# Empty TensorE instructions taken out of a fused RWKV6 and shrink layer, and one more pair of tiles joined in block 2

## The chip, the cores and the metric

One core of one Trainium2 chip runs the whole kernel. The metric is the device time of one launch in microseconds (us). Five engines work side by side, each with its own stream of instructions: TensorE (PE) multiplies, its weight loads are listed apart as PEld, VectorE is DVE, ScalarE is ACT, GpSimd is POOL, and SyncE (SP) issues DMAs. A q behind an engine's name (PEq, SPq) is its sequencer.

## The reference, cut to what matters

```python
# attention: B, H, S, D = 4, 8, 768, 48
for t in range(S):
    cur = u * k[t] (outer) v[t]
    y[t] = r[t] @ (state + cur)
    state = w[t][:, None] * state + k[t] (outer) v[t]
x = y as (B*S, H*D)            # 3072 tokens x 384
h = x @ w_in                   # 384 x 2048
g = h - tanh(h)
out = g @ w_out                # 2048 x 384
```

All tensors are float32.

## The kernel before, in words

The 3072 tokens are cut into 8 blocks of 384 (a batch and a half of its sequence). The attention of block i + 1 is worked out while the two dense layers of block i run; block 0's own attention comes first, in a stage of some 25 us. The dense layers of a block are 16 tiles f of 128 hidden units, and the main loop (from L1346) goes over the blocks and the tiles.

A tile, as a rule:
- `first` (L893): three float32 matmuls of 128x384 on PE (L895) into the one PSUM tile `hp`. A float32 matmul runs as two passes on PE, each with its own weight load, so it is four instructions of PE's stream.
- `slight` (L972 and on): for small h, h - tanh(h) is made as a product of two tanh. ACT makes them (L984, L985), and a square that is summed for a later test (L988).
- DVE multiplies them to g (L902) and makes sums and differences of pieces of g (L1007) for the second layer.
- `Fewer.add` (L1088): the second layer, for two tiles (a pair) at a time, as products of 128x128 of such forms. Part 0 of a pair takes products 8, 9, 10, 11, 6, 7, part 1 takes 0 to 5; they are due two and three tiles after the pair's second tile. Of a pair's ten forms DVE makes 0 to 3 at once and holds back 4 to 9 (two in one L1007), which only part 1 needs. Behind a joined pair 1, forms 6 and 7 of pair 0 stand right behind the product g (L902) of tile 3 in DVE's order, and 8 and 9 two places further on.

A pair of tiles can instead be **joined** (`Twos.begin`, L958): eleven float32 matmuls of 128x192 in place of twelve, which need forms of the weights (`weight_forms`, L934, the tile `kept`) and of the block's tokens (`token_forms`, L942, the tile `turned`). Their results are put together by one copy of ACT (L959) and four additions of DVE (L968), and then `slight` runs on both tiles from the SBUF tile `joint`. `JOINED` lists the joined pairs of each block, `PAIRS` and `FORMED` where their weight forms are made: the key is (block, tile), the value the set and the order of its five forms.

Between the tiles stand pieces of the next block's attention. Three of them are bursts of many small matmuls on PE: the scores "earlier" (L504), the "update" of the states (L585), and the results "together" (L781), near the end of each block: 352 or 384 instructions, alternately. The decays of a block are running products along time, made on DVE as scans: "behind" (L439, with `take_whole`, L459), and "before" (L426, L427), each for halves "2" and "0" of the heads. `plan(i)` (L1142 to L1193) says at which tile of block i each of these steps stands: `phases` for PE's steps, `before` for steps of block i + 1, `ahead` for steps of block i + 2, and `loads` for the DMAs, whose issue is made to stand behind the tanh of its tile. In block 0 the k of block 2 is loaded at tile 13 (L379), just ahead of the L781 burst; in blocks 1 and 3 to 5 its r is loaded a tile or two ahead of that burst.

The order of instructions on PE, DVE, ACT and SP is the order in which the program writes them (a manual schedule); only the waits between engines are put in by the framework.

`first` also takes a count `apart`: so many empty instructions (NOP, L898) are put on PE behind each of its matmuls. `SPACED` has two counts for each block, for its tiles up to 12 (13 in blocks 0 and 1) and for those behind. Other empty instructions (L1042) stand in block 0's second layer.

## Time and profile before

| what | value |
|---|---|
| median of 3 runs | 537.61 us (536.98 to 539.62) |
| the profiled execution | 538.27 us, of which the span of the trace is 536.4 us |
| PE's granted clock, mean of the span | 0.995 |
| DVE, ACT busy | 462.5 us (86%), 310.3 us (58%) |
| bytes moved | 56.33 MB, mean 105 GB/s |

Times inside the trace count from the start of the span. The page's line "q8 instruction" is the DMA queue that brings instructions. In a row of a timeline stand the start, the duration, the engine, the line, the operation, what it writes and reads, its shape and the count of equal instructions that were put in one row; in brackets the idle time of the engine before it, and what ended it. A windows row has a stretch, its length, and for each engine the busy time with its count, then the granted clock of PE, the DMA share and GB/s. A DMA answer has 40 digits, the busy share of the 16 DMA engines in 40 equal slots of the stretch asked for (a packet is put where it starts), and the queues' packets, megabytes and share.

### The profile page before, as it was taken

To read this page: it belongs to the slowest core of one execution; us is meant where nothing else is said; L and a number is where in the kernel's file an instruction comes from. 1 tells how busy PE (TensorE), PEld (TensorE's weight loads), DVE (VectorE), ACT (ScalarE), POOL (GpSimd) and SP (SyncE) were. 2 spreads that over 40 slices of the span, in tenths; PEclk is the share of its full clock that TensorE was granted. 3 is DMA by queue.
4 is the path that set the end of the run, shared out by engine and by line. 5 is a ranking of instruction groups with operands and counts; after the bars stand their busy time and mean duration, and the time that the engine had idled before them with its cause. 6 is when DMAs were issued, how large, how long until landed. Compare 5 with 4: busy or idle time off the path is not lost.

```text
span 536.4 us, 14922 instructions
## 1 busy us (share of the span) xinstructions
PE 526.9 (98%) x5950; PEld 437.5 (82%) x5950; DVE 462.5 (86%) x970; ACT 310.3 (58%) x720; POOL 9.1 (2%) x57
## 2 busy tenths in 40 slices
PE   8899999999999999999999999999999999999996
PEld 5756666677887889889789898899888897899994
DVE  7899897699979889988998899988999889667874
ACT  4899984666445573555655475374735655435450
POOL 1100000000000000000000000000000000000001
PEclk9899999999999999999999999999999999999999
DMA  8698733252302622162313722146221510100011
GB/s 280 224 404 333 241 105 109 89 148 61 120 13 89 163 74 89 51 137 82 120 57 75 178 60 68 50 90 165 63 90 39 140 40 2 56 1 2 11 34 47
DMA packets 53046, 56.33 MB, mean 105 GB/s; under 512 B 21488, under 2 KB 50928, under 8 KB 52976
## 3 DMA queue, kind: packets, MB, share of 16 engines
q1 hardware_dynamic: 52592, 55.18, 34.2%
q8 instruction: 49, 0.80, 0.7%
q14 instruction: 21, 0.17, 0.1%
q10 hardware_dynamic: 288, 0.10, 0.1%
q0 software_dynamic: 96, 0.07, 0.1%
HBM read 44.73 MB, written 4.72 MB: 92 GB/s over the span
## 4 chain that ended last, share of the span: by engine, by line
PE 96%; DMA 1%; issue 1%; ACT 0%; DVE 0%; SPq 0%; PEldq 0%; PEld 0%; DVEq 0%
PE acc L1088 27%; PE hp L895 27%; PE att L958 17%; PE acc L1039 6%; PE att L781 4%; PE hp L1088 3%; PE att L1088 3%; PE att L504 3%; PE att L585 2%; PE acc L1066 1%; PE att L895 1%; DMA r<-in_rT 1%; PE acc L895 1%; PE att L527 1%; PE att L689 1%
## 5 line engine op out<-in xcount | busy, mean ns | idle before, releaser
L895 PE MATMUL hp<-xT,w_sb 128*128 128x384 f32 x438 | 154.3, 488 | 0.7 <-issue 0.7
L1088 PE MATMUL acc<-forms,g 128*128 128x128 f32 x972 | 135.9, 276 | 0.0
L1088 PEld LDWEIGHTS acc<-forms,g 128*128 128x128 f32 x972 | 124.0, 192 | 4.3
L895 PEld LDWEIGHTS hp<-xT,w_sb 128*128 128x128 f32 x438 | 78.6, 190 | 43.5 <-issue 0.9
L1007 DVE TENSOR_TENSOR g<-g 128x256 f32<-128x256 f32 x270 | 107.1, 419 | 4.6 <-PE acc L1088 0.3
L984 ACT ACTIVATE h<-hp 128x384 f32<-128x384 f32 x73 | 35.9, 492 | 96.8 <-PE hp L895 96.8
L902 DVE SCALAR_TENSOR_TENSOR g<-h,qa 128x384 f32<-128x384 f32 x112 | 61.7, 551 | 21.8 <-ACT h L988 21.4
L988 ACT ACTIVATE h<-h 128x384 f32<-128x384 f32 x113 | 58.7, 519 | 0.0
L1088 PE MATMUL acc<-w_sb,g 128*128 128x128 f32 x324 | 54.1, 276 | 0.0
L958 PE MATMUL att<-xT,w_sb 128*128 128x192 f32 x250 | 53.0, 326 | 0.0
L1088 PEld LDWEIGHTS acc<-w_sb,g 128*128 128x128 f32 x324 | 46.4, 192 | 5.5
L968 DVE TENSOR_TENSOR joint<-joint,att 128x384 f32<-128x384 f32 (+1 forms) x72 | 34.6, 501 | 18.0 <-PE att L958 11.0
L984 ACT ACTIVATE h<-joint 128x384 f32<-128x384 f32 x36 | 18.7, 518 | 39.7 <-DVE joint L968 39.7
L958 PEld LDWEIGHTS att<-xT,w_sb 128*128 128x128 f32 x250 | 41.4, 190 | 0.0
L985 ACT ACTIVATE qa<-hp 128x384 f32<-128x384 f32 x73 | 35.7, 489 | 0.0
L1123 DVE TENSOR_TENSOR sums<-sums 128x256 f32<-128x256 f32 x84 | 32.9, 410 | 1.4 <-ACT sums L1100 0.9
L1039 PE MATMUL acc<-w_sb,sums 128*128 128x384 f32 x96 | 33.7, 487 | 0.0
L271 ACT ACTIVATE up<-raw 128x768 f16<-128x768 f32 (+1 forms) x32 | 32.7, 1093 | 0.0
L1039 PEld LDWEIGHTS acc<-w_sb,sums 128*128 128x128 f32 x96 | 18.1, 190 | 12.3
L427 DVE TENSOR_TENSOR_SCAN pre<-w,start 128x780 f32<-128x780 f32 x14 | 25.0, 1782 | 0.8
L439 DVE TENSOR_TENSOR_SCAN post<-w,seed 128x780 f32<-128x780 f32 x14 | 24.9, 1775 | 0.0
L958 PE MATMUL att<-turned,kept 128*128 128x192 f32 x126 | 23.9, 326 | 0.0
(157 smaller groups left out, 768.3 us busy)
## 6 DMA issues: line engine op xcount, KB each, us to landing
raw<-in_weights SPq DMA_DIRECT2D x16, 768.0 KB, 6.4
w<-in_wT SPq DMA_DIRECT2D x7, 780.0 KB, 5.4
k<-in_kT SPq DMA_DIRECT2D x7, 768.0 KB, 4.5
r<-in_rT SPq DMA_DIRECT2D x7, 768.0 KB, 4.4
v_sb<-in_v SPq DMA_DIRECT2D x8, 576.0 KB, 4.1
k<-in_tokens SPq DMA_DIRECT2D x7, 576.0 KB, 4.2
r<-in_tokens SPq DMA_DIRECT2D x7, 576.0 KB, 4.9
out_y<-sums SPq DMA_DIRECT2D x18, 128.0 KB, 1.9
```

What stands on the lines that cost most here:

```text
L271: return lambda: nc.scalar.activation(out=to, in_=of, func=AF.Copy, scale=scale, bias=bias)
L895: nc.tensor.matmul(hp, lhsT=w_in_sb[:, f, kc, :], rhs=xT[kc], start=(kc == KC - 1), stop=(kc == 0))
L902: return lambda: nc.vector.scalar_tensor_tensor(out=out, in0=in0, scalar=scalar, in1=in1, op0=op0, op1=ALU.mult)
L958: nc.tensor.matmul(to, lhsT=lhs, rhs=rhs, start=n == 0, stop=n + 1 == len(of))
L968: return [lambda of=of: nc.vector.tensor_tensor(out=of[0], in0=of[1], in1=of[2], op=ALU.add) for of in ((h[:, 0:5:4], twice(h[:, 3]), both ...
L984: made = nc.scalar.activation(out=t, in_=h, func=AF.Tanh, scale=INNER / UPSCALE)
L985: nc.scalar.activation(out=by, in_=h, func=AF.Tanh, scale=OUTER / UPSCALE)
L988: nc.scalar.activation(out=t, in_=t, func=AF.Square, accum_out=top[:, n:n + 1])
L1007: return lambda: nc.vector.tensor_tensor(out=G[:, to:to + 2], in0=two(G, g_at(q, a0), g_at(q, a1)), in1=two(G, g_at(q, b0), g_at(q, b1)), ...
L1039: nc.tensor.matmul(acc, lhsT=g[:, j * P:(j + 1) * P], rhs=w_out_sb[:, f, :], start=(f == self.first), stop=(f == NF - 1))
L1088: nc.tensor.matmul(to, lhsT=G[:, g_at(q, a), :], rhs=rhs, start=start, stop=stop, skip_group_check=True)
L1123: ops.append(lambda op=op, at=at: nc.vector.tensor_tensor(out=at[0], in0=at[1], in1=at[2], op=OPS[op]))
```

## The change

- `SPACED` and the count `apart` go: the 483 empty instructions behind the matmuls of `first` are no longer made. Those of L1042 stay.
- Pair 1 (tiles 2 and 3) is joined in block 2 as well. Its weight forms are made at tile 8 of block 1, those of pair 7 at tile 5 of block 2, and those of pairs 3 and 4, which stood at tile 8 of block 1, at tile 6 of block 2. The token forms of block 2 are made at its tile 0.
- The scan "behind 0" with `take_whole` moves from tile 0 of block 2 to tile 15 of block 1, and the scan "before 2" from tile 2 to tile 1 of block 2. "before 0" stays at tile 3, where it stood.
- In block 2 the phases that split scores are not moved up behind a joined pair (`near and i > 2`).

```diff
-SPACED = (3, 0), (0, 3), (3, 2), (2, 3), (3, 2), (2, 3), (3, 0), (0, 0)
...
-JOINED = {2: (4, 7), 3: BESIDE, 4: BESIDE, 5: BESIDE, 6: BESIDE, 7: TWOS}
+JOINED = {2: (1, 4, 7), 3: BESIDE, 4: BESIDE, 5: BESIDE, 6: BESIDE, 7: TWOS}
 PAIRS = range(1, 2), range(3, 5), range(7, 8)
...
-FORMED = {(1, 8): (1, (0, 2, 1, 4, 3)), (1, 15): (0, (0, 2, 1, 4, 3)), (2, 6): (2, (0, 2, 1, 4, 3)),
+FORMED = {(1, 8): (0, (0, 2, 1, 4, 3)), (2, 5): (2, (0, 2, 1, 4, 3)), (2, 6): (1, (0, 2, 1, 4, 3)),
...
-    def first(xT, f, hp, apart=0):
+    def first(xT, f, hp):
         for kc in reversed(range(KC)):
             nc.tensor.matmul(hp, lhsT=w_in_sb[:, f, kc, :], rhs=xT[kc],
                              start=(kc == KC - 1), stop=(kc == 0))
-            for _ in range(apart):
-                nc.tensor.nop(nofuse=True, hint="apart")
         return hp
...
-            ahead = {12: ("bound 2",), 13: ("behind 2", "take_whole 2"), 14: ("bound 0",)}
+            ahead = {12: ("bound 2",), 13: ("behind 2", "take_whole 2"), 14: ("bound 0",),
+                     15: ("behind 0", "take_whole 0")}
...
-            before = {0: ("behind 0", "take_whole 0", "times_behind 2"), 1: ("times_behind 0",), 2: ("before 2",),
-                      3: ("before 0",), 4: ("times_before", "held"), 5: ("product_u",), 7: ("product_r",),
+            before = {0: ("times_behind 2",), 1: ("times_behind 0", "before 2"), 3: ("before 0",), 4: ("times_before", "held"), 5: ("product_u",), 7: ("product_r",),
...
-                h = first(here, f, to[:, 0:NB], SPACED[i][f > 12 + (i < 2)])
+                h = first(here, f, to[:, 0:NB])
...
-                if near:
+                if near and i > 2:
...
-            if later and i in JOINED and f == (i == 2) or i == blocks_n - 2 and f == 14:
+            if later and i in JOINED and not f or i == blocks_n - 2 and f == 14:
```

Line numbers of the changed kernel are lower: by one from L80 to L895 or so, by three behind `first`.

PE in block 0, the last tile ahead of the L781 burst, which follows four rows further on. Before, each matmul of the first layer is followed by three empty instructions:

```order
L895 MATMUL hp<-xT_134,w_sb 128x384
L898 NO_OP x3
L895 MATMUL hp<-xT_133,w_sb 128x384
L898 NO_OP x3
L895 MATMUL hp<-xT_132,w_sb 128x384
L898 NO_OP x3
L1039 MATMUL acc_131<-w_sb,sums 128x384
L1042 NO_OP
```

The same place of PE's stream now:

```order
L894 MATMUL hp<-xT_134,w_sb 128x384
L894 MATMUL hp<-xT_133,w_sb 128x384
L894 MATMUL hp<-xT_132,w_sb 128x384
L1036 MATMUL acc_131<-w_sb,sums 128x384
L1039 NO_OP
```

Nothing but the empty instructions went, so what follows stands nine places earlier in the stream for each such tile.

PE in block 2, from pair 1 (tiles 2 and 3) to the scores burst. Before, the two tiles and those behind them run one by one; these are the end of tile 4, part 1 of pair 0, tile 5 and the burst (`hp` is written by the first layer, the three `acc` by the second):

```order
L895 MATMUL hp<-xT_1315,w_sb 128x384
L898 NO_OP x3
L1088 MATMUL acc_131<-forms,g 128x128 x4
L1088 MATMUL acc_602<-w_sb,g 128x128
L1088 MATMUL acc_602<-forms,g 128x128
L895 MATMUL hp<-xT_1317,w_sb 128x384
L898 NO_OP x3
L895 MATMUL hp<-xT_1316,w_sb 128x384
L898 NO_OP x3
L895 MATMUL hp<-xT_1315,w_sb 128x384
L898 NO_OP x3
L504 MATMUL att_126<-pre,post 64x64 x24
```

Now, from the end of part 0 of pair 0 on (the eleven matmuls of the joined pair stand six rows ahead of the first row):

```order
L1085 MATMUL acc_602<-forms,g 128x128 x2
L894 MATMUL hp<-xT_1191,w_sb 128x384
L894 MATMUL hp<-xT_1190,w_sb 128x384
L894 MATMUL hp<-xT_1189,w_sb 128x384
L1085 MATMUL acc_131<-forms,g 128x128 x4
L1085 MATMUL acc_602<-w_sb,g 128x128
L1085 MATMUL acc_602<-forms,g 128x128
L894 MATMUL hp<-xT_1191,w_sb 128x384
L894 MATMUL hp<-xT_1190,w_sb 128x384
L894 MATMUL hp<-xT_1189,w_sb 128x384
L503 MATMUL att_126<-pre,post 64x64 x24
```

Part 1 of pair 0 (the three L1085 rows in the middle) stands behind tile 4 and ahead of tile 5, and the scores burst behind tile 5, both as before; ahead of them, eleven shorter matmuls stand in the place of tiles 2 and 3.

DVE, from tile 15 of block 1 into tile 1 of block 2. Before (L902 is the product g of a tile, L1007 its forms):

```order
L902 SCALAR_TENSOR_TENSOR g<-h,qa 128x384
L439 SCALAR_TENSOR_TENSOR post<-w,seed 128x780
L1007 TENSOR_TENSOR g<-g 128x256
L459 TENSOR_SCALAR whole<-post 128x12
L453 TENSOR_TENSOR post<-k,post 128x768
L902 SCALAR_TENSOR_TENSOR g<-h,qa 128x384
L1007 TENSOR_TENSOR g<-g 128x256 x4
L1115 SCALAR_TENSOR_TENSOR sums<-att_125,o 128x384
L453 TENSOR_TENSOR post<-k,post 128x768
L942 TENSOR_TENSOR turned<-xT_1315 128x192
```

Now:

```order
L438 SCALAR_TENSOR_TENSOR post<-w,seed 128x780
L458 TENSOR_SCALAR whole<-post 128x12
L899 SCALAR_TENSOR_TENSOR g<-h,qa 128x384
L452 TENSOR_TENSOR post<-k,post 128x768
L1004 TENSOR_TENSOR g<-g 128x256
L939 TENSOR_TENSOR turned<-xT_1189 128x192
L939 TENSOR_TENSOR turned<-xT_1190,xT_1189 128x192
L939 TENSOR_TENSOR turned<-xT_1190,turned 128x192 x2
L899 SCALAR_TENSOR_TENSOR g<-h,qa 128x384
L1004 TENSOR_TENSOR g<-g 128x256 x4
```

The scan (the row that writes `post` from `w` and `seed`) now stands ahead of the product g of block 1's last tile, in the place of pair 1's weight forms, and the token forms (`turned`) stand a tile earlier.

## The prediction

> **What bounds the kernel now.** I read the page first, then the waits of PE, the timeline around its two holes, the DMA answers of the same moments, and at last the places that the change touches.

> ```profile
> PE 526.9 (98%) x5950; PEld 437.5 (82%) x5950; DVE 462.5 (86%) x970; ACT 310.3 (58%) x720; POOL 9.1 (2%) x57
> q8 instruction: 49, 0.80, 0.7%
> PE 96%; DMA 1%; issue 1%; ACT 0%; DVE 0%; SPq 0%; PEldq 0%; PEld 0%; DVEq 0%
> ```

> PE is busy for 98% of the span and holds 96% of the chain that ended last, so a gain must shorten PE's own work and a loss must open a hole in it. The waits of PE behind the first layer's start show two holes that no engine explains; "issue" means that nothing visible was waited for:

> ```profile
> PE att L504 <- issue: 1.5, 1, 1.5
> PE hp L895 <- issue: 0.7, 1, 0.7
> ```

> The timeline of PE shows the second (start, duration, operation). The L781 burst of block 6 is followed by one pass of tile 13, whose 384 columns last 0.32 us from start to start, and then by nothing until 458.25: about 0.9 us lost.

> ```profile
> 454.18 1.56 PE L781 MATMUL att<-pre,states 48*48 48x64 f32 x96
> 455.56 1.52 PE L781 MATMUL att<-scores,v_sb 64*48 64x64 f32 x96
> 457.01 0.59 PE L895 MATMUL hp<-xT,w_sb 128*128 128x384 f32 x1
> 458.25 1.45 PE L895 MATMUL hp<-xT,w_sb 128*128 128x384 f32 x4 [0.66 <-issue]
> ```

> Ahead of it lies one packet of the instruction queue. The DMA answer for 455.70 to 455.90 (40 slots of 5 ns) has it in slot 20, at 455.80, and 32.0% of 16 engines for 0.2 us are 1.02 us: it ended at 456.82, and PE went on 1.43 us later.

> ```profile
> DMA  0000000000000000000900000000000000000000
> q8 instruction: 1, 0.02, 32.0%
> ```

> The first hole ends in the same way. In 18.50 to 18.70 the packet stands in slot 15, at 18.57; 35.7% of 3.2 us are 1.14 us, so it ended at 19.71, and PE went on at 21.15, which is 1.44 us later.

> ```profile
> DMA  0000000000000090000000000000009990009090
> q8 instruction: 1, 0.02, 35.7%
> ```
> ```profile
> 21.15 0.50 PE L504 MATMUL att<-pre,post 48*64 48x64 f32 x18 [1.51 <-issue]
> ```

> So PE waits for code. 0.80 MB in 49 fetches are 16.4 KB each, and the distance of the two holes says how many instructions that is. Between them the windows view counts 4968 matmul passes and 4969 weight loads, and the two lines of empty instructions (NOP) have all of theirs there:

> ```profile
> 21.15:458.25 437.10, 436.45 (x4968) 357.15 (x4969) 390.03 (x803) 264.57 (x612) 2.69 (x31) 1.00 0.38 113
> L898 PEldq NOP  x483: 13/13/13, 24.3 to 451.3; - x161
> L1042 PEldq NOP  x33: 13/13/13, 31.0 to 74.9; - x33
> ```

> **The law of a page.** The two L781 rows and the L895 row behind them give 2.83 us for 384 instructions (192 passes, 192 loads), 7.37 ns each. Counting, page ends lie at instruction 131 of block 6's burst and just behind its last. PE passed the former at 454.18 + 131 x 0.00737 = 455.15; the page after it could be used at 458.25, 3.1 us later. A page that lies wholly in a burst is eaten in 256 x 0.00737 = 1.89 us, which leaves a hole of 3.1 - 1.89 = 1.2 us. Outside the bursts a pass of 128 columns and its load take 114 ns (24 of them from 291.00 to 293.73 in the rows of part 2), 57 ns an instruction, and a page lasts many times 3.1 us. So only where the page ends lie in the L781 bursts counts. Before, the end that matters is over 30 instructions behind the burst in blocks 2 to 5, and no hole is seen there.

> **Part 1: the 483 empty instructions.** In place they cost PE nothing. Tiles in block 1 (none) and block 2 (three behind each matmul):

> ```profile
> 135.99 2.10 PE L895 MATMUL hp<-xT,w_sb 128*128 128x384 f32 x6
> 137.92 1.05 PE L1088 MATMUL acc<-forms,g 128*128 128x128 f32 x8
> ```
> ```profile
> 176.13 2.10 PE L895 MATMUL hp<-xT,w_sb 128*128 128x384 f32 x6
> 178.07 1.05 PE L1088 MATMUL acc<-forms,g 128*128 128x128 f32 x8
> ```

> From L895 to the next product it is 1.93 us without and 1.94 us with them. What they do is shift the pages. Counted in the new list, page ends fall at these instructions of the bursts: block 0 at 73 and 329 (before: 203); block 1 at 15 and 271; block 2 at 165, and 37 behind its end; block 3 at 176, and 80 behind; block 4 just ahead and at 251; block 5 at 6 and 262; block 6 at 81 and 337.

> Block 6: both ends are now inside, so the hole is 1.2 us where it was 0.9: **+0.3**.

> Block 0: by the law alone +1.2. But the load of k is issued just ahead of this burst:

> ```profile
> 77.91 0.38 SPq L379 DMA_DIRECT2D k<-in_kT  x1
> 78.37 1.56 PE L781 MATMUL att<-pre,states 48*48 48x64 f32 x96
> 79.75 1.52 PE L781 MATMUL att<-scores,v_sb 64*48 64x64 f32 x96
> 81.20 2.20 PE L895 MATMUL hp<-xT,w_sb 128*128 128x384 f32 x6
> ```

> The fetch that belongs to the end at 203 was due at 78.37 + 203 x 0.00737 + 0.65 = 80.5 (0.65 being 455.80 - 455.15). The DMA answer for 81.70 to 81.85 has it in slot 22, at 81.78, where k's packets run out (q1 fills the slots until then):

> ```profile
> DMA  9909000019000100190900900090000000990000
> q8 instruction: 1, 0.02, 39.9%
> ```

> It waited 1.3 us for the bulk load. In the changed kernel the fetch is due at 78.37 + 73 x 0.00737 + 0.65 = 79.6, in the midst of that load; started at 81.78 as well, it ends at 82.75 and is usable at 84.2, while PE needs it at 78.37 + 329 x 0.00737 = 80.8. The hole is **3.4 us**. The ends are 1.2 (no waiting) and 3.4; I take 3.4, since the delayed fetch was seen in this very load.

> Blocks 1, 4 and 5: the first end lies at the burst's start, where each instruction of lead of the sequencer is worth 57 ns, so 22 of them would hide the 1.2 us. But the load of r fills the DMA up to the burst; block 1, 138.60 to 142.60, and its burst:

> ```profile
> DMA  0000000000136619674296999999999999999743
> ```
> ```profile
> 142.63 0.55 PE L781 MATMUL att<-scores,v_sb 64*48 64x64 f32 x24
> ```

> A fetch that starts at the burst's start, behind the load, is usable 1.0 + 1.44 = 2.4 us in; PE needs it after 271, 251 and 262 instructions, at 2.0, 1.85 and 1.93 us. That is 0.4, 0.6 and 0.5, **+1.5** together; the ends are 0 and 3 x 1.2 = 3.6.

> The clock: in the two stretches behind the 1.5 us hole at 20 us, the granted clock (the column behind the count) is about half for some 3.5 us:

> ```profile
> 22.00:24.00 2.00, 2.00 (x64) 0.59 1.04 371
> 24.00:26.00 2.00, 2.00 (x35) 0.56 0.95 361
> ```

> If block 0's hole brings the same, 2.00 x 0.41 + 2.00 x 0.44 = 1.7 us of PE's work is lost. Behind the 0.9 us hole it did not happen. Ends 0 and 1.7; I take the middle, **+0.8**. [...]

> **Part 2: pair 1 joined in block 2.** Block 3 joins the same pair already, and its rows have every step (the timeline of PE, then of DVE):

> ```profile
> 287.42 1.14 PE L958 MATMUL att<-xT,w_sb 128*128 128x192 f32 x6
> 291.00 1.05 PE L1088 MATMUL acc<-forms,g 128*128 128x128 f32 x8
> 293.73 2.10 PE L895 MATMUL hp<-xT,w_sb 128*128 128x384 f32 x6
> 295.76 1.63 PE L504 MATMUL att<-pre,post 48*64 48x64 f32 x96
> 297.32 1.16 PE L1088 MATMUL acc<-forms,g 128*128 128x128 f32 x8
> 296.30 0.56 DVE L902 SCALAR_TENSOR_TENSOR g<-h,qa 128x384 f32<-128x384 f32 x1 [0.21 <-ACT h L988]
> 296.78 1.09 DVE L1007 TENSOR_TENSOR g<-g 128x256 f32<-128x256 f32 x3
> ```

> The joined pair takes 291.00 - 287.42 = 3.58 us against 2 x 1.94 for two tiles: **-0.3**. What comes late is part 1 of pair 0: its third product reads forms that DVE makes behind tile 3's product. The chain runs over the copies, the tanh of both tiles, L902 and the first of the three L1007, which ends at 296.78 + 0.42 = 297.20 (three that start 0.34 apart take 1.09), 9.78 us behind the pair's start. In block 3 the L504 burst of 1.56 us stands between tile 4 and part 1 and hides the wait. In block 2 that burst comes a tile later, so PE arrives at part 1 295.76 - 287.42 = 8.34 us after the start, does two products (four passes of 114 ns, 8.80), and stands until 9.78; the last L1007 ends 0.67 us later, which two more products (0.46) do not cover, 0.2 more. I take **+1.2** (ends 0, if block 2's shorter queues bring the chain forward, and 1.5). Behind the waiting product on PE stand only tile 5 and the L504 burst; nobody else is late for it.

> DVE gets the pair's four L968 (about 2 us), the pair's forms move to other tiles, and the two scans go earlier. The tightest receiver is the second pair of block 2, whose forms are ready at 179.55 and read at 183.66:

> ```profile
> 179.26 0.29 DVE L934 TENSOR_TENSOR kept<-w_sb,kept 128x128 f32<-128x128 f32 x1
> 183.66 1.14 PE L958 MATMUL att<-turned,kept 128*128 128x192 f32 x6
> ```

> The 2 us added ahead of it fit into these 4.1 us, and no DMA moves: 0. Were that cover gone, the price would be what exceeds 4.1 us.

> **The sum:** 3.4 + 1.5 + 0.3 + 0.8 - 0.3 + 1.2 = +6.9 us on the profiled execution's 538.27 us (span 536.4), 545.2. The median shown is 537.61, 0.66 lower, so I predict **544.5 us**.

> **Rivals.**
> Fetches are not held up by loads: block 0 loses 1.2, blocks 1, 4 and 5 nothing, block 6 +0.3, block 2 +0.9, the clock perhaps 0.8. That is +2.4 to +3.2, 540.0 to 540.8. For it speaks that the load of k is issued only just ahead of the fetch; against it, the packet at 81.78.
> Not slower: the sequencer runs so far ahead that all fetches are hidden. Then 0.9 of block 6 goes and block 2's 0.9 comes: 537.6. For block 0 it decides from a lead of about 73 + 22 = 95 instructions. Against it: block 6's end at 131 left a hole of 0.9. [...]
> The empty instructions cost PE time after all: 483 x 13 ns (L898's own row) are 6.3 us, 531.3 us or a little more. Against it: 1.93 beside 1.94.

> **How the numbers follow.** Forecast 0.58, fetches not held up 0.22, hidden 0.15, empty instructions on PE 0.02, worse than all this (a clock lost in several places) 0.03. The forecast's own range is 541.9 to 547.0: all ends of blocks 1, 4 and 5, clock and wait together would give more at either side, but not at once. Reaching to the case of fetches that are not held up, the range is 540.0 to 547.0. A measurement tells about 0.5% from no change, 2.7 us, so "same" is 534.9 to 540.3: 0.15 and a part of the second case.

> **What would show it.** PE's waits list "issue" at L781 in block 0 (about 80.8 to 84.2) and block 6, small ones in blocks 1, 4 and 5, none at L895 behind block 6's burst; a wait of L1088 for DVE g L1007 in block 2 between tiles 4 and 5; a half clock behind block 0's hole or not; each hole ends 1.44 us behind a packet of the instruction queue. Without the L781 holes the count or the law is wrong; with block 0's hole at 1.2 us the hold-up is.

## The result, and the profile after

| | before | changed |
|---|---|---|
| median of 4 runs each, us | 538.26 (536.98 to 539.62) | 545.95 (544.09 to 546.80) |
| profiled execution, us (span) | 538.27 (536.4) | 544.09 (542.4) |
| ratio of the runs | | 1.0138 (1.0100 to 1.0176) |

The change costs 7.7 us between the medians. The profiled execution of the changed kernel is the fastest of its four (the others took 1.8 to 2.7 us longer, at mean granted clocks of 0.991 to 0.995 against its 0.997), so its trace shows less, 6.0 us of span. By the starts of the results bursts (L781, now L780), in the two traces:

| stretch | before, us | changed, us | difference |
|---|---|---|---|
| start to block 0's burst | 78.37 | 76.62 | -1.75 |
| to block 1's | 64.26 | 69.10 | +4.84 |
| to block 2's | 60.32 | 61.65 | +1.33 |
| to block 3's, to block 4's | 125.61 | 125.61 | 0 |
| to block 5's | 62.85 | 63.33 | +0.48 |
| to block 6's | 62.77 | 63.31 | +0.54 |
| to the end of the span | 82.22 | 82.78 | +0.56 |

The first row is no part of the change, whose first removed instruction stands behind block 0's own attention (the boot, some 25 us): the hole at 20 us, 1.5 us before, was 0.4 us in this execution, and no half clock followed it. Without it the rows add up to 7.75 us, close to what the medians show.

The page of the changed kernel, the rows that were shown of before (PE, the instruction queue, the chain):

```profile
PE 527.8 (97%) x5960; PEld 439.5 (81%) x5960; DVE 464.3 (86%) x974; ACT 310.2 (57%) x721; POOL 9.1 (2%) x57
q8 instruction: 48, 0.79, 0.6%
PE 94%; DVE 1%; issue 1%; ACT 1%; DMA 1%; SPq 0%; PEldq 0%; PEld 0%; DVEq 0%
```

PE does nearly the same work in nearly the same busy time (526.9 us before); what was added is idleness. PE's waits, without those of the first microseconds (line, what was waited for, us in all, times, the longest):

```profile
PE att L780 <- issue: 4.6, 4, 3.1
...
PE acc L1085 <- DVE g L1004: 1.0, 1, 1.0
PE att L503 <- issue: 0.4, 1, 0.4
```

Four holes now lie inside results bursts, where before there was none, the hole at L895 behind block 6's burst is gone, and PE waits once for DVE's forms. The timeline of PE around block 0's burst, and the two rows of the DMA answer for 79.75 to 79.95:

```profile
77.78 0.40 PE L780 MATMUL att<-pre,states 48*48 48x64 f32 x16
78.01 1.19 PE L780 MATMUL att<-scores,v_sb 64*48 64x64 f32 x68
82.30 1.09 PE L780 MATMUL att<-scores,v_sb 64*48 64x64 f32 x28 [3.10 <-issue]
83.32 3.17 PE L894 MATMUL hp<-xT,w_sb 128*128 128x384 f32 x6
```
```profile
DMA  8009898099909009199098999008809891192800
q8 instruction: 1, 0.02, 31.7%
```

The answer's GB/s row has the packet in slot 19, at 79.84; it took 1.01 us, and 1.45 us after its end PE went on. 68 passes of the second half were done, 164 of the burst's 192, so the hole stands at instruction 329 of the burst, as counted ahead. The other queue's packets (q1, the load of k) fill the slots up to there.

The clock was at half for 3.4 us, from 81.90, still inside this hole, to 85.3 (windows of PE: stretch, length, busy and count, granted clock):

```profile
82.00:83.00 1.00, 0.70 (x26) 0.50 0.00 0
83.00:84.00 1.00, 1.00 (x13) 0.50 0.08 16
84.00:85.00 1.00, 1.00 (x3) 0.50 0.00 0
85.00:86.00 1.00, 1.00 (x3) 0.84 0.10 25
```

The three matmuls of the tile behind the burst last 3.17 us in place of 2.20 in this place before, and the burst's last 28 passes are stretched by some 0.4 more: by these rows the half clock costs 1.4 us. By the stretch, 4.84 less the hole's 3.3, it is 1.5.

The same timeline at the three other holes:

```profile
335.17 1.21 PE L780 MATMUL att<-scores,v_sb 64*48 64x64 f32 x67 [0.18 <-issue]
398.70 0.98 PE L780 MATMUL att<-pre,states 48*48 48x64 f32 x45 [0.21 <-issue]
461.00 1.19 PE L780 MATMUL att<-scores,v_sb 64*48 64x64 f32 x72
463.30 0.55 PE L780 MATMUL att<-scores,v_sb 64*48 64x64 f32 x24 [1.10 <-issue]
```

The count of what was left says where they are: 67 of 192 passes in block 4 (instruction 250), 45 of 176 in block 5 (262), 24 of 192 in block 6 (336). A row's bracket is shorter than what was lost, since the ends of matmuls are modelled: from start to start block 4's hole is 0.4 us, block 6's 1.3.

And the wait in block 2, between tile 4 and tile 5:

```profile
172.72 0.61 PE L1085 MATMUL acc<-forms,g 128*128 128x128 f32 x4
174.30 0.71 PE L1085 MATMUL acc<-forms,g 128*128 128x128 f32 x4 [0.97 <-DVE g L1004]
174.97 0.49 PE L1085 MATMUL acc<-w_sb,g 128*128 128x128 f32 x2
175.52 2.10 PE L894 MATMUL hp<-xT,w_sb 128*128 128x384 f32 x6
```

Two products run, the third waits, and the three behind it come at DVE's pace: 2.80 us from the first to the next tile, where 12 passes of 114 ns make 1.37.

### The profile page after: what moved, and what is told of

It reads as the page before. It is cut to its first block, busy times and chain, and to the rows that moved or that the text cites. A ratio compares the mean times of both kernels' runs of the same rounds, so it can differ in the third digit from the quotient of the medians.

```text
span 542.4 us, 14457 instructions
## 1 busy us (share of the span) xinstructions
PE 527.8 (97%) x5960; PEld 439.5 (81%) x5960; DVE 464.3 (86%) x974; ACT 310.2 (57%) x721; POOL 9.1 (2%) x57
## 4 chain that ended last, share of the span: by engine, by line
PE 94%; DVE 1%; issue 1%; ACT 1%; DMA 1%; SPq 0%; PEldq 0%; PEld 0%; DVEq 0%
PE acc L1085 27%; PE hp L894 25%; PE att L955 17%; PE acc L1036 6%; PE att L780 4%; PE hp L1085 3%; PE att L1085 3%; PE att L503 2%; PE att L584 2%; PE acc L1063 1%; PE att L894 1%; DMA r<-in_rT 1%; PE acc L894 1%; PE att L526 0%; PE att L688 0%
## 5 line engine op out<-in xcount | busy, mean ns | idle before, releaser
L894 PE MATMUL hp<-xT,w_sb 128*128 128x384 f32 x426 | 150.9, 491 | 0.0
L1085 PE MATMUL acc<-forms,g 128*128 128x128 f32 x972 | 136.3, 276 | 1.0 <-DVE g L1004 1.0
L1085 PEld LDWEIGHTS acc<-forms,g 128*128 128x128 f32 x972 | 124.1, 192 | 5.1 <-DVE g L1004 1.2
L894 PEld LDWEIGHTS hp<-xT,w_sb 128*128 128x128 f32 x426 | 77.0, 192 | 42.2 <-issue 0.9
L955 PE MATMUL att<-xT,w_sb 128*128 128x192 f32 x260 | 55.1, 326 | 0.0
L1085 PE MATMUL acc<-w_sb,g 128*128 128x128 f32 x324 | 54.2, 276 | 0.0
L965 DVE TENSOR_TENSOR joint<-joint,att 128x384 f32<-128x384 f32 (+1 forms) x76 | 36.5, 501 | 18.1 <-PE att L955 11.3
L1085 PEld LDWEIGHTS acc<-w_sb,g 128*128 128x128 f32 x324 | 46.3, 192 | 5.4
L955 PEld LDWEIGHTS att<-xT,w_sb 128*128 128x128 f32 x260 | 43.1, 190 | 0.0
L981 ACT ACTIVATE h<-joint 128x384 f32<-128x384 f32 x38 | 19.7, 519 | 39.9 <-DVE joint L965 39.9
L955 PE MATMUL att<-turned,kept 128*128 128x192 f32 x132 | 25.0, 326 | 0.0
```

The lines of the kernel that those rows point to most:

```text
L894: nc.tensor.matmul(hp, lhsT=w_in_sb[:, f, kc, :], rhs=xT[kc], start=(kc == KC - 1), stop=(kc == 0))
L955: nc.tensor.matmul(to, lhsT=lhs, rhs=rhs, start=n == 0, stop=n + 1 == len(of))
L965: return [lambda of=of: nc.vector.tensor_tensor(out=of[0], in0=of[1], in1=of[2], op=ALU.add) for of in ((h[:, 0:5:4], twice(h[:, 3]), both ...
L981: made = nc.scalar.activation(out=t, in_=h, func=AF.Tanh, scale=INNER / UPSCALE)
L1085: nc.tensor.matmul(to, lhsT=G[:, g_at(q, a), :], rhs=rhs, start=start, stop=stop, skip_group_check=True)
```

## The experiments

The theory, from the counts of the trace before: PE's code is fetched in pages of 256 instructions (10,496 of them in 41 fetches; the DMA answer for 18.5 to 455.9 us has 42 packets of the instruction queue q8, those of the two holes first and last), a page in a results burst is eaten in 1.89 us, faster than the next could be used (3.1 us at block 6), and the empty instructions did nothing but keep the page ends out of the bursts. The rivals: the joined pair and its moved work are the loss; the empty instructions had some effect of their own; the load of k, or the fetch, is late for another reason. Line numbers move by a few from kernel to kernel.

### Each half of the change alone

`no_empty` is the kernel before with all counts of `SPACED` at zero:

```diff
-SPACED = (3, 0), (0, 3), (3, 2), (2, 3), (3, 2), (2, 3), (3, 0), (0, 0)
+SPACED = (0, 0), (0, 0), (0, 0), (0, 0), (0, 0), (0, 0), (0, 0), (0, 0)
```

> The kernel before without the 483 empty instructions, no pair more joined. Page theory: page ends fall at instructions 73 and 329 of block 0's results burst, 15 and 271 in block 1, 16 and 272 in block 4, 27 and 283 in block 5, 102 and 358 in block 6. Holes of PE with nothing visible waited for: 3.1 us in block 0 and a half clock behind it (1.7 us more), 0.1 in block 1, 0.4 in blocks 4 and 5, 1.2 in block 6 in place of 0.9 behind the burst. Together 5.5 to 6.5 us above the kernel before. If the loss came from the joined pair, it is gone here: within 0.5 us of before. If the empty instructions kept PE busy in some other way (spacing, power), the loss is spread over the tiles of all blocks and no hole ends behind an instruction fetch.

`join_only` is the changed kernel with `SPACED` and the NOPs of `first` put back:

```diff
+SPACED = (3, 0), (0, 3), (3, 2), (2, 3), (3, 2), (2, 3), (3, 0), (0, 0)
...
-                h = first(here, f, to[:, 0:NB])
+                h = first(here, f, to[:, 0:NB], SPACED[i][f > 12 + (i < 2)])
```

> The changed kernel with the empty instructions back as they were (18 fewer, since the joined tiles have no first layer of that form). Page theory: page ends lie as in the kernel before (196 in block 2, 159, 162, 125, and 128 with the next just behind the burst in block 6), so the only holes are block 6's 0.9 to 1.1 us and the wait of block 2's products for DVE's forms, 1.0 us; with 0.3 saved by the joined pair 0.7 to 1.0 us above the kernel before. If the joined pair and its moved scans are the loss, 5 to 8 us above.

Measured: `no_empty` 544.03 us against 538.40, ratio 1.0113 (1.0091 to 1.0136), 5.6 us. `join_only` 539.39 us, 1.0017 (1.0004 to 1.0030), 1.0 us. PE's waits of `no_empty`, and below them those of `join_only`:

```profile
PE att L781 <- issue: 4.4, 3, 3.1
```
```profile
PE hp L895 <- ACT xT L753: 1.2, 1, 1.2
PE acc L1088 <- DVE g L1007: 1.0, 1, 1.0
PE att L781 <- issue: 0.5, 1, 0.5
```

The two halves give 6.6 us, 5.6 and 1.0, beside 7.7 for the whole; the 1.1 us between them lie within the interval of the whole (1.0100 to 1.0176, or 5.4 to 9.5 us). Without the empty instructions the holes are in the bursts; with them the forms' wait stays and the rest is, but for one burst, as before. (The wait put down to ACT's `xT` is block 6's hole behind the burst, which ends at the first matmul that reads `xT`.) One thing was not foreseen: `join_only` has 0.8 us more in block 2's burst, at its page end at 196, which lay at 199 before without a hole. Block 2 loads its r ahead of the burst as well. In `join_only` the fetch started at 204.24, 0.25 us ahead of the burst, as r's load (issued at 200.50) ran out; before, the fetch had started (198.62) when the load was issued (198.96).

### Block 0 alone: the page end, and the load

`shift_b0` puts 126 empty instructions ahead of block 0's burst and 130 behind it, so that all later page ends stand where the changed kernel has them:

```diff
+EMPTY = {(0, f): 9 for f in range(16)}
+EMPTY.update({(1, f): 9 for f in range(12)})
+EMPTY[1, 12] = 4
...
+            for _ in range((empty + kc) // KC):
+                nc.tensor.nop(nofuse=True, hint="apart")
```

> The changed kernel with 126 empty instructions ahead of block 0's results burst and 130 behind it, 256 together, so that every page end behind stands where it was. Page theory: block 0's page end moves from 329 to 203 of the burst, its hole of 3.1 us and the half clock behind it go, and all other holes stay: 4.5 to 5 us below the changed kernel, 2.5 to 3 above the kernel before. If the load of k alone were at fault, wherever the page ends, nothing changes. If the empty instructions worked by themselves, half of them would bring back about half of the loss, spread over blocks 0 and 1.

`k_early` leaves the pages and issues block 0's load of k a tile earlier:

```diff
-            loads.update({2: "next r", 11: "w", 13: "k", 14: "r"})
+            loads.update({2: "next r", 11: "w", 12: "k", 14: "r"})
```

> The changed kernel with the load of k in block 0 issued at tile 12 in place of tile 13, so that its packets are through before the fetch for instruction 329 of the burst is due. If the fetch is held up by that load, block 0's hole shrinks from 3.1 to the 1.2 us that a page inside a burst leaves, and the half clock behind it may go: 1.9 to 3.5 us below the changed kernel. If the fetch is late for another reason, the hole stays at 3.1 us and the time within 0.5 us of the changed kernel.

Measured: `shift_b0` 539.93 us, ratio to before 1.0026 (1.0011 to 1.0041), which is 6.0 us below the changed kernel's median. `k_early` 541.47 us, 1.0058 (1.0037 to 1.0079), 4.5 below it. The timeline of PE at block 0's burst, of `shift_b0` and of `k_early`, and the clock of `k_early` behind the hole:

```profile
79.00 1.52 PE L783 MATMUL att<-scores,v_sb 64*48 64x64 f32 x96
80.45 2.20 PE L897 MATMUL hp<-xT,w_sb 128*128 128x384 f32 x6
```
```profile
79.41 1.18 PE L780 MATMUL att<-scores,v_sb 64*48 64x64 f32 x68
81.80 0.65 PE L780 MATMUL att<-scores,v_sb 64*48 64x64 f32 x28 [1.21 <-issue]
82.38 2.20 PE L894 MATMUL hp<-xT,w_sb 128*128 128x384 f32 x6
```
```profile
82.00:84.00 2.00, 2.00 (x33) 1.00 0.03 8
```

With the page end at 203 there is no hole, though the load of k holds that fetch up too: in `shift_b0` it started at 81.22, where the law would have had it at 79.8. With the page end at 329 and the load out of the way the fetch starts as the law has it (79.27, beside 79.2), and a hole is left 68 passes into the half as in the changed kernel: 1.4 us from start to start, beside the law's 1.2, and the clock stays whole. From block 0's burst to block 1's it is 64.26 us in `shift_b0`, as in the kernel before, 65.79 in `k_early` and 69.10 in the changed kernel: 3.3 us of hole and 1.5 of half clock became 1.5 and nothing. The medians show some 1.2 us more than these 4.8 and 3.3, and so more than was expected of both runs; that is less than the 1.75 us by which the start of the program alone differs between the two traces above. So both are needed: the page end makes 1.5 us, and the load of k stretches it to 3.3.

### Block 2: whose turn it is on DVE

`forms_first` takes pair 0's held-back forms ahead of tile 3's product in block 2:

```diff
+            elif carried and i == 2:
+                ops, carried = carried + between(rest + formed, behind + spare), []
             elif carried:
                 ops, carried = between(rest + formed, carried + behind + spare), []
```

> The changed kernel, but in block 2 DVE makes the held-back forms of pair 0 ahead of tile 3's product in place of between and behind it; nothing else moves, and all page ends stay. If PE waits there for forms that stand behind a product whose tanh is late, the wait of 1.1 us and the trickle of 0.3 us behind it go: 1.2 to 1.5 us below the changed kernel. If the forms are late for the joined pair's load on DVE or ACT as such, the wait moves to the next product and less than 0.5 us is gained.

Measured: 545.48 us, ratio 1.0136 (1.0119 to 1.0153); by time no difference from the changed kernel can be told. PE's wait in block 2, and DVE's timeline ahead of it:

```profile
PE att L503 <- DVE pre L445: 0.5, 1, 0.5
```
```profile
176.20 0.42 DVE L1120 TENSOR_TENSOR sums<-sums 128x256 f32<-128x256 f32 x1
176.54 0.42 DVE L1004 TENSOR_TENSOR g<-g 128x256 f32<-128x256 f32 x1
176.87 0.42 DVE L1120 TENSOR_TENSOR sums<-sums 128x256 f32<-128x256 f32 x1
177.21 1.75 DVE L445 TENSOR_TENSOR pre<-r,pre 128x1536 f32<-128x1536 f32 x1
```

The wait for the forms is gone, but the scores burst, which PE now reaches 1.1 us earlier, waits 0.5 us for DVE's product of r with its decays. From block 1's burst to block 2's the trace shows 61.14 us, 0.5 less than the changed kernel's 61.65 and 0.8 more than before. Neither theory was right by itself: the first wait was one of order, and behind it stood a second one.

### Versions that place the page ends

`before_b6` moves one page end of the kernel before:

```diff
-SPACED = (3, 0), (0, 3), (3, 2), (2, 3), (3, 2), (2, 3), (3, 0), (0, 0)
+SPACED = (3, 0), (0, 3), (3, 2), (2, 3), (3, 2), (2, 3), (1, 0), (0, 0)
```

> The kernel before with one empty instruction in place of three behind each first-layer matmul of block 6, tiles up to 12: 42 fewer. The page end just behind block 6's burst moves to 45 instructions behind it, like that of block 4 (37). Page theory: the hole of 0.9 us at tile 13 goes and no other appears: 0.9 us below the kernel before. If that hole belongs to the tile or to the burst's end, it stays.

`placed` is `forms_first` with a table of its own:

```diff
+EMPTY = {(0, f): 10 for f in range(14)}
+EMPTY.update({(2, f): 13 for f in (0, 1, 4, 5, 6, 7, 10, 11, 12)})
+EMPTY.update({(4, f): 12 for f in (0, 1, 4, 5, 10, 11, 12)})
+EMPTY.update({(6, f): 12 for f in (0, 1, 4, 5, 10, 11, 12)})
```

> The changed kernel with the forms of block 2 moved as in forms_first, and 425 empty instructions in blocks 0, 2, 4 and 6 (10 to 13 a tile) placed so that the page ends lie between instructions 131 and 189 of each burst and 35 to 81 behind its end. Page theory: no hole in any results burst and no wait in block 2: the joined pair's 0.3 and block 6's 0.9 us below the kernel before, some 536.5 to 537.5 against 538.4. If the empty instructions cost time by their number, it is as slow as before or slower.

`placed_boot` also shifts the pages of the first 25 us:

```diff
-        own = blk.own(ps, h1, spare=94, ahead=5, late=6)
+        own = blk.own(ps, h1, spare=110, ahead=5, late=6)
...
-EMPTY = {(0, f): 10 for f in range(14)}
+EMPTY = {(0, f): 8 for f in range(14)}
```

> As placed, but with 16 more small filler matmuls at the very start, where PE waits anyway, and 28 fewer empty instructions in block 0: in the first 25 us the page ends come 32 instructions earlier in the code, which leaves about 4.3 us for each page in place of 3.4, and later bursts keep theirs to within 4 instructions. If the hole at 20 us is a page that is eaten too fast, it shrinks from 1.0 to 1.8 us to under 0.8, and the half clock behind it does not come: 0.5 to 1.5 us below placed. If the fetches there wait for the loads in any case, the hole stays.

`placed_sums` is `placed` with two sums of block 2 a tile later:

```diff
+            if i == 2 and f in (4, 5):
+                some = (0, 2) if f == 5 else None
             spare = summed[0].sum(*some) if some else []
```

> As placed, and in block 2 DVE's two sums of the previous block's results stand a tile later, so that the product of r with its decays, for which the scores burst waited 0.5 us in placed, comes 1.0 us earlier. If DVE's order is all that costs the joined pair its gain, the wait goes, 0.3 us of trickle stays against the joined pair's 0.3: 0.5 us below placed, about 1 us below the kernel before. If DVE is simply full there, the wait moves on to the next burst or product and the time is that of placed.

`placed_plain` is the kernel before, without the pair, with a table of the same kind (10 for each tile of block 0 up to 13; 12, 10 and 11 for each tile up to 12 of blocks 2, 4 and 6 that isn't joined):

> The kernel before, with no pair more joined, and 419 empty instructions placed so that page ends lie between 131 and 197 of each burst and 35 to 101 behind its end; in block 2 at 170, farther from the load of r than 199. If page ends are all that the empty instructions are for, PE has no hole behind 25 us: 0.9 us below the kernel before, 0.1 to 0.4 below the kernel with block 6 alone mended, and level with placed_sums. If their place among the tiles matters, new holes or waits appear.

| kernel | median, us | ratio to before, 95% |
|---|---|---|
| before_b6 | 536.90 | 0.9979 (0.9968 to 0.9990) |
| placed | 537.24 | 0.9989 (0.9979 to 0.9999) |
| placed_boot | 538.07 | 1.0010 (0.9998 to 1.0021) |
| placed_sums | 536.95 | 0.9974 (0.9963 to 0.9986) |
| placed_plain | 537.39 | 0.9979 (0.9966 to 0.9992) |

The timeline of PE of `before_b6`, at block 2's burst and at block 6's:

```profile
205.03 1.55 PE L781 MATMUL att<-scores,v_sb 64*48 64x64 f32 x93 [0.58 <-issue]
...
456.28 1.52 PE L781 MATMUL att<-scores,v_sb 64*48 64x64 f32 x96
457.73 1.56 PE L895 MATMUL hp<-xT,w_sb 128*128 128x384 f32 x4
```

Block 6's hole is gone for 42 empty instructions less, 0.8 us in the trace (4.87 us in place of 5.68 from the burst's start to the products behind the tile) and 1.1 us in the ratio. But this execution has a hole of 0.8 us at 199 in block 2's burst, where the kernel before, with the same code up to there, had none. The load of r was issued 3.99 us ahead of the burst in both traces; the fetch started 4.33 us ahead of the burst before, and 0.04 us ahead of it here, when the load was through. What made it late was not found. `placed_plain`, with its end at 170, has none there, and one of 0.4 us at 186 in block 4.

`placed` has no hole in any burst with 425 empty instructions: they cost nothing by their number. It still has the wait of the scores burst, 0.5 us, and `placed_sums` is rid of that; its list of PE's waits begins, and ends, in the boot:

```profile
PE att L322 <- POOL ident masks.py:199: 2.1, 1, 2.1
PE att L507 <- issue: 1.6, 1, 1.6
PE att L507 <- ACT k L467: 1.3, 1, 1.3
```

From block 1's burst to block 2's it takes 60.53 us, where before took 60.32, so the joined pair's gain is eaten even here. It is lost in part 1 of pair 0: from its first product to the next tile PE takes 1.79 us (168.55 to 170.34) where it took 1.34 before (169.76 to 171.10), while DVE makes the last three forms from 168.45 to 169.74. `placed_sums` is the best of all, 1.4 us below the kernel before by its ratio; it can't be told from `before_b6` or `placed_plain`. `placed_boot` gained nothing: the hole at 20 us shrank to 0.6 us and no half clock followed, but another hole of 1.4 us came at 24.75, and the time is 0.8 us above `placed`. What sets the fetches of the first 25 us, where the windows of `placed_boot` from 16 to 26 us have a DMA share of 0.53 to 0.99, was not found.

## Why the prediction was right, and where it was off

Forecast 544.5 us (540.0 to 547.0); measured 545.95. Of the 1.45 us between them 0.65 come from the start of the sum, a median before of 537.61 us from three runs, which is 538.26 with the fourth. The rest is in the terms, in us, measured in the traces:

| term | forecast | measured |
|---|---|---|
| hole in block 0 | 3.4 | 3.3 |
| half clock behind it | 0.8 | 1.5 |
| blocks 1, 4, 5 | 0.4, 0.6, 0.5 | 0.1, 0.5, 0.5 |
| block 6, above its hole of before | 0.3 | 0.5 |
| joined pair and the wait of part 1 | -0.3, +1.2 | +1.2 together |
| sum | 6.9 | 7.6 |

- **What bounds it, the law of a page.** Right. Every hole that the page count gave came, and the four that can be placed stand at the instruction it gave, each ending 1.4 to 1.5 us behind an instruction packet; block 1's 0.1 us shows only as a longer row. Most page ends showed no hole (49 fetches and two such holes in the trace before); where a page is eaten within a burst, these runs show 0.1 to 3.3 us a crossing.
- **The empty instructions cost nothing in place, and were worth 5.6 us by where they stood.** Shown by `no_empty` for the loss (544.03 us against 538.40) and by `placed` and `placed_sums` for the cost (537.24 and 536.95 us with 425 of them).
- **The fetch held up by a load.** Shown for block 0 by `k_early` (a hole of 1.4 us in place of 3.3) with the page ends left alone. For blocks 1, 4 and 5 it is argued: their fetches started 0.22, 0.18 and 0.03 us ahead of the burst, as r's load ran out, which fits, but no run moved r's load. Block 1's hole was forecast at 0.4 and was 0.1, since its fetch started those 0.22 us earlier than assumed and took 0.88 us in place of 1.0.
- **The half clock** was the term most off, 0.8 taken as the middle of 0 and 1.7, 1.5 measured. Within block 0's burst it came with 3.3 us of hole and not with the 1.4 of `k_early`, so there it is a price of the hold-up, not of the page end alone. That the forecast took neither end was a choice without a reading behind it.
- **The joined pair.** The wait was where it was put, between tiles 4 and 5, for the forms. Its size was set a little low: the first product waited 1.1 us where 1.0 was forecast, and the three behind it came 0.3 us late at DVE's pace where 0.2 was, 1.4 us in all by the passes (2.80 against 1.37) and not 1.2. What was costed at nothing, DVE's moved and added work, was not free: `forms_first` uncovered a second wait of 0.5 us, which the first had hidden, and the forecast did not see it.
- **The rivals.** That all fetches are hidden, that none is held up, and that the empty instructions occupy PE would have given 537.6, 540.0 to 540.8 and 531.3; the holes, `k_early` and `placed` speak against them in this order.

## What to carry to other kernels

In this kernel bursts of very short instructions (7.37 ns each on PE) lost 0.1 to 3.3 us each to the fetch of their code where a page was eaten within them, and the place of a page's end in a burst was decided by every instruction that stood ahead of it: an edit that only removed empty instructions cost 5.6 us (`no_empty`), in bursts many tiles on. The sign of it was idle time that waited for nothing visible and ended 1.4 to 1.5 us behind a packet of the instruction queue. The remedy here was to count the page ends, to place them where no page is eaten within a burst, with empty instructions among longer work, where they cost nothing (`placed`: 425 of them, 537.24 us), and to keep the bulk load from being issued just ahead of the fetch (`k_early`: 4.5 us below the changed kernel). Where another kernel's trace shows the same sign, its page ends can be counted in the same way. An added saving on the engine that bounds the kernel is only worth what the order on the others allows, so each wait that is removed should be asked for the next one behind it.

## What the runs showed of the hardware that was not expected

- The length of a hole alone did not say whether the half clock came: at about 20 us it came behind holes of 1.5 us (before), 1.5 (`k_early`), 1.8 (`join_only`) and 1.1 (`placed`), and not behind 0.4 (the changed kernel), 1.0 (`no_empty`), 1.4 (`shift_b0`) or 1.6 (`placed_sums`). Where the windows show its whole length it lasted 3.4 us: at about 20 us in before, `k_early`, `placed`, `placed_plain` and `forms_first`, and behind block 0's hole in the changed kernel and in `forms_first`. What else decides was not found.
- In these traces a fetch that was due while a bulk load was queued started as the load ran out: at 79.84 in the changed kernel, where the law would have had it at 77.8 (0.65 us behind instruction 73), and at 81.78 in the kernel before, where it was due at 80.5. The one that had started before its load was issued (198.62 before 198.96) was not touched. With the same code and the same place of the load, that fetch was early in one execution and some 4 us later in another (`before_b6`, 202.75), and with it a hole of 0.8 us at 199 in block 2 came or did not.
